# Decode attention over a sliding block of cache: V per group in 64 KB rows, one batch from each of two queues

## The chip, the cores and the metric

One core of a Trainium2 chip. The metric is device time in microseconds of one execution. The kernel before takes 363.2 us (median of 3 runs, 363.07 to 363.21).

## The reference

Two independent problems, A and B, each one decode step of an attention layer, with the results side by side:

```python
B, Sq, D = 2, 1, 576
Hq, Hkv, Sk, Dh = 32, 16, 16384, 128        # W = 4096, rep = Hq // Hkv = 2
q = (x @ wq).reshape(B, Sq, Hq, Dh)          # then heads ahead of Sq
k = repeat(k_cache[:, :, Sk - W:, :], rep)   # the last 4096 positions
v = repeat(v_cache[:, :, Sk - W:, :], rep)
p = softmax(q @ k^T * Dh ** -0.5)
out = (p @ v).reshape(B, Sq, Hq * Dh) @ wo   # 576 columns for each problem
```

All tensors are bf16. K and V of the window are 134 MB in all, wq and wo 9.4 MB each. There is one query row for each head and batch, so every byte of K and V is used for two query heads only.

## The kernel before

**Groups and slabs.** The 16 K/V heads of a problem are taken four at a time: four groups for a problem, eight in all (`NG`), numbered G. A slab is one group, one batch, K or V: 128 partitions of 32 KB, 4,096 KB in all. A partition holds 128 successive positions (`KJ`) of one head, so the 4096 positions of a head lie on 32 partitions. There are 16 K slabs (t = 2G + batch) and 16 V slabs (i likewise).

**Transfers.** `ring` has four slots of one slab. A list `stream` gives the order, K0 K1 K2 K3 V0 K4 V1 and so on, with the output weights (`wo`) as M pieces for groups 0 to 5 and W pieces for the last two. All go from SyncE's queue (L380 for slabs, L364 for wo), each after the last reader of its slot. The last V slab is read in two pieces, the last wo in three.

**Work on a K slab.** `make_X` (L432) turns half a slab in 32 x 32 blocks on DVE into `xt` (two halves, jh = 0 and 1). `make_S` (L442) multiplies it on PE by `zq`, a block layout of the queries that `make_Z` (L414) writes on POOL, into the score tile `st` of the group; a half is 16 matmuls of 512 columns (L462 and, with the weights held, L266). Both batches add into the same tile.

**Softmax of a group.** `make_max` (L468) takes the row maximum on DVE and picks the valid ones on POOL; `make_Tm_pe` (L475) turns it to a row on PE; `make_nM` (L480) reduces it on DVE and scales it on POOL; `make_bias` (L489) turns it back on PE, makes four biases on DVE, and runs four exponentials on ACT (L500), one for each of the four K/V heads, with the sums. `make_pT` (L506) turns the result on DVE into `pT`, which has two buffers. `make_rsum` and `make_sums` (L514, L518) add up the sums and take the reciprocal.

**Work on a V slab.** `make_PV` (L544, matmuls L539) multiplies the V slab by columns of `pT`, as 32 matmuls on tiles of 128 x 32, four of which take the columns of the array side by side. `make_evac` (L553) scales the product out of PSUM and reduces it (L562, L569) on DVE. `make_dg` (L573) on PE and `make_pick` (L582) on DVE bring a group's rows into the layout for the output product, `make_projm` and `make_proj` (L622, L645), whose result `make_E` (L675) writes out.

**Order.** Each engine runs its steps in the order in which the code names them, and waits by semaphores for the others. The loop at L700 goes over K slabs, and what belongs to a group is spread over the slabs that follow, with V three slabs behind K (`LAG`): in the turn of an even t it names X(t,0), the evacuation of V slab t-4, the pick and the maximum of group t/2-1, X(t,1), the row maximum and bias of that group, and the V product of slab t-3; in the turn of the odd t after it X(t,0), an evacuation, pT of that group, X(t,1), its sums, and a V product. So on DVE an X stands between a group's bias and its pT. L741 to L770 write the tail by hand, with `filler` matmuls that compute nothing.

Of the kernel before, what the change touches and what calls it, by code (L numbers as in the profile page):

```python
# [63 lines left out]
def build_kernel(nc, probs, out):  # L64
    NSLOT = 4
    LAG = 3
# [27 lines left out]
    with es:  # L94
# [5 lines left out]
        pR = sb("pR", [128, 2048], BF16)  # L100
        pT = sb("pT", [128, 2, 2048], BF16)
        tmp = sb("tmp", [128, 512], FP32)
        oR = sb("oR", [128, Bb, 128], FP32)
# [4 lines left out]
        ones_f = sb("ones_f", [128, 128], FP32)  # L108
        ones_b = sb("ones_b", [128, 128], BF16)
        sel = sb("sel", [128, 4, 128], BF16)  # L110
        bmask = sb("bmask", [128, 4], FP32)
        vmask = sb("vmask", [128, 4], FP32)
        offm = sb("offm", [128, 4], FP32)
# [4 lines left out]
        m8 = sb("m8", [128, 16, 8], FP32)  # L118
        selx = sb("selx", [128, 8, 16], FP32)
        selm = sb("selm", [128, 16, 8], FP32)  # L120
        bsel = sb("bsel", [128, 2], FP32)
        hmask = sb("hmask", [4, 2], FP32)
        mx = sb("mx", [128, 2], FP32)
        mv = sb("mv", [128, 2], FP32)
        m1 = sb("m1", [128, 1], FP32)
        nM = sb("nM", [1, 16], FP32)
        nMrep = sb("nMrep", [1, 8, 16], FP32)
        bias4 = sb("bias4", [128, 4], FP32)
        rsum4 = sb("rsum4", [128, 4], FP32)
        rsum8 = sb("rsum8", [128, 2, 4], FP32)  # L130
        ssum = sb("ssum", [128, 2], FP32)
        rsb = sb("rsb", [128, 2, 2], FP32)
# [3 lines left out]
        out_w = sb("out_w", [32 + Bb, NH], BF16)  # L136
# [12 lines left out]
        pTf = pT[:].rearrange("p v f -> p (v f)")  # L149
# [3 lines left out]
        assert XW + 512 <= 2 * 2048  # L153
# [5 lines left out]
        ring_sem = [sem("ring%d" % r) for r in range(NSLOT)]  # L159
        v_cuts = [0, 80, KJ]  # L160
        lastv_sem = [sem("lastv")]
# [61 lines left out]
        def turn_x(P):  # L223
# [5 lines left out]
            def f_xT(e, P=P):  # L229
                for k in range(4):  # L230
# [8 lines left out]
        d_dm = mask(dmask[:, 0:4], ident_f[:].rearrange("p (c j q) -> p j c q", j=4, q=8), AX.XY, "dmask")  # L239
# [4 lines left out]
        p_offm = pool(lambda e: e.tensor_scalar(offm[:], vmask[:], -1.0, OFF, ALU.add, ALU.mult), [d_vm], "offm")  # L244
        p_v2 = pool(lambda e: e.tensor_tensor(v2[:], vmask[:, 0:2], vmask[:, 2:4], ALU.add), [d_vm], "v2")
        p_m8 = pool(lambda e: e.tensor_copy(m8[:], jmask_f[:, 0:8].unsqueeze(1).broadcast_to([128, 16, 8])), [d_jf], "m8")
        p_sx = pool(lambda e: e.tensor_copy(selx[:], jmask_f[:, 0:8].unsqueeze(2).broadcast_to([128, 8, 16])), [d_jf], "selx")
        p_sm = pool(lambda e: e.tensor_copy(selm[:].rearrange("p (a h) c -> p a h c", a=2),
                                            jmask_f[:, 0:8].unsqueeze(1).unsqueeze(3).broadcast_to([128, 2, 8, 8])), [d_jf], "selm")
# [72 lines left out]
        stream = []  # L322
        for t in range(NSLAB + LAG):
            if t < NSLAB:
                stream.append(("K", t))
            if t >= LAG:
                i = t - LAG
                if i % 4 == 0 and i > 0:
                    stream.append(("M", i // 4 - 1))
                stream.append(("V", i))  # L330
        stream.append(("W", NG - 2))
        stream.append(("W", NG - 1))
        NM = NG // 2 - 1
        slot_of = {}
        uses = {}
        n_slot = 0
        for key in stream:
            if key[0] in "KV":
                slot_of[key] = (n_slot + 3) % NSLOT
                uses.setdefault(slot_of[key], []).append(key)  # L340
                n_slot += 1
        first_deps = {0: [q_done[0]], 1: [q_done[0], q_done[1]], 2: [q_done[1]], 3: []}
        stream_dma = {}
        last_reader = {}
# [4 lines left out]
        def issue(key):  # L349
# [18 lines left out]
            P, g, b = i // (2 * GP), (i // 2) % GP, i % 2  # L368
            src_t = probs[P][1] if kind == "K" else probs[P][2]
            src = src_t[b, 4 * g:4 * g + 4, Sk - W:Sk, :].rearrange("k (r j) d -> r k j d", j=KJ)  # L370
            r = slot_of[key]
            prior = uses[r][:uses[r].index(key)]
            deps = [last_reader[prior[-1]]] if prior else first_deps[r]
            cuts = [(0, KJ, ring_sem[r])]
            if key == ("V", NSLAB - 1):
                cuts = [(v_cuts[k], v_cuts[k + 1], ([ring_sem[r]] + lastv_sem)[k]) for k in range(2)]
            stream_dma[key] = []
            for c0, c1, sm in cuts:
                def f(e, c0=c0, c1=c1, sm=sm):
                    return e.dma_start(ring[:, r, c0 * 128:c1 * 128],  # L380
                                       src[:, :, c0:c1, :].rearrange("r k j d -> r k (j d)")).then_inc(sm, 16)
                stream_dma[key].append((c0, c1, dma_op("sp", sm, 1, f, deps, "%s%d_%d" % (kind, i, c0))))
# [6 lines left out]
        def filler(n):  # L389
            def f(e):  # L390
                o = STT[(NG - 1) % 2][:, 0:512]
                last = e.matmul(o, ones_b[:, :], xt[:, 0, 0:512], start=True, stop=True, skip_group_check=True)
                for _ in range(n - 1):
                    last = mm_held(e, o, ones_b[:, :], xt[:, 0, 0:512], True)
                return last
            pe(f, [exp_op[NG - 1], Xop[(NSLAB - 1, 1)]], "filler")
# [17 lines left out]
        def make_Z(t):  # L414
            P, g, b = t // (2 * GP), (t // 2) % GP, t % 2
            deps = [qs_ev, p_zq, d_bm]
            if t >= 2:
                deps.append(Sop[(t - 2, 1)])

            def f(e):  # L420
                for kp in range(2):
                    m = 2 * b + kp
                    b0 = zq[:, 0, m, 16 + 4 * m:16 + 4 * m + 1]
                    dst = bass.AP(b0.tensor, b0.offset, [list(b0.ap[0]), [4 * 144, 4], [32, 4], [1, 4]])
                    o = b * Hq + 8 * g + 4 * kp
                    src = qs[:, P, :].rearrange("d (p w) -> d p w", p=4)[:, :, o:o + 4].unsqueeze(2).broadcast_to([128, 4, 4, 4])
                    msk = bmask[:, 0:4].unsqueeze(1).unsqueeze(3).broadcast_to([128, 4, 4, 4])
                    last = e.tensor_tensor(dst, src, msk, ALU.mult)  # L428
                return last
            Zop[t] = pool(f, deps, "Z%d" % t)  # L430

        def make_X(t, jh):  # L432
            ensure(("K", t))
            r = slot_of[("K", t)]
            deps = [stream_dma[("K", t)][0][2], Sop[(t - 1, jh)] if t >= 1 else d_xT[1]]
# [6 lines left out]
        def make_S(t, jh):  # L442
# [3 lines left out]
            if b == 0 and G >= 2:  # L446
                deps.append(exp_op[G - 2])
# [32 lines left out]
        def make_nM(G):  # L480
            n, b = tm_job[G]
            op = ch[(G, "Tm")]
            nm = dve(lambda e: e.tensor_reduce(nM[0:1, 0:16], b[0:1, 0:128].rearrange("o (a w) -> o w a", a=8), AX.X, ALU.max, negate=True),
                     [op] + prev(G, "nMrep"), "nM%d" % G)
            tb_consumer[n] = nm
            ch[(G, "nMrep")] = pool(lambda e: e.tensor_scalar(nMrep[:], nM[0:1, 0:16].unsqueeze(1).broadcast_to([1, 8, 16]), SCALE, None, ALU.mult),
                                    [nm] + prev(G, "bias"), "nMrep%d" % G)

        def make_bias(G):  # L489
            n, bk, op = tb_job(lambda e, bank: e.transpose(bank[:, 0:1], nMrep[0:1].rearrange("o a w -> o (a w)"), ident_f[0:1, 0:1]),  # L490
                               "bias%d" % G, [ch[(G, "nMrep")], p_ident_f])
            ch[(G, "bias")] = op
            b4 = dve(lambda e: e.scalar_tensor_tensor(bias4[:], vmask[:], bk[:, 0:1], offm[:], ALU.mult, ALU.add),  # L493
                     [op, p_offm, d_vm] + ([exp_op[G - 1]] if G >= 1 else []), "bias4_%d" % G)
            tb_consumer[n] = b4
            st = STT[G % 2]

            def f(e):
                for kv in range(4):
                    last = e.activation(pR[:].rearrange("p (x k) -> p k x", k=4)[:, kv, :],  # L500
                                        st[:, :].rearrange("p (x t) -> p t x", t=2)[:, kv % 2, :], ACTF.Exp,
                                        bias=bias4[:, kv:kv + 1], scale=SCALE, accum_out=rsum4[:, kv:kv + 1])
                return last
            exp_op[G] = act(f, [b4] + prev(G, "rsum8") + ([pT_op[G - 1]] if G >= 1 else []), "exp%d" % G)

        def make_pT(G):  # L506
            v = G % 2
            deps = [exp_op[G]] + ([PVop[2 * (G - 2) + 1]] if G >= 2 else [qt_op])
            pT_op[G] = dve(lambda e: e.transpose(  # L509
                pT[:, v, :].rearrange("p (w j q) -> p j w q", w=4, q=8),  # L510
                pR[:].rearrange("p (j w q) -> p j w q", w=4, q=8)), deps, "pT%d" % G)

        def make_rsum(G):
            ch[(G, "rsum8")] = pool(lambda e: e.tensor_tensor(  # L514
# [348 lines left out]
```

## Time and profile before

| | us |
|---|---|
| device time, median of 3 runs | 363.2 |
| device time of the profiled execution | 363.1 |
| span of its instructions | 361.8 |
| PE busy | 229.0 (63%) |
| DVE busy | 218.6 (60%) |
| ACT busy | 45.4 (13%) |
| POOL busy | 24.3 (7%) |
| mean granted TensorE clock | 0.887 |
| moved, mean rate over the span | 153.28 MB, 424 GB/s |

The span runs from the first instruction to the last; the device time has 1.3 us more around it. Busy times are sums over the whole span and don't tell which engine sets the pace of a stretch. A group of instructions is named by line, engine and operation, then what it writes and reads, the shapes and the count; behind it stand the busy time, the mean of one in ns, the idle time before them and who ended it. Matmuls are pipelined and their ends are modelled, so the starts of successive ones tell more than their lengths.

### The profile page before, as it was taken

To read this page: it belongs to the slowest core of one execution; us is meant where nothing else is said; L and a number is where in the kernel's file an instruction comes from. 1 tells how busy PE (TensorE), PEld (TensorE's weight loads), DVE (VectorE), ACT (ScalarE), POOL (GpSimd) and SP (SyncE) were. 2 spreads that over 40 slices of the span, in tenths; PEclk is the share of its full clock that TensorE was granted. 3 is DMA by queue.
4 is the path that set the end of the run, shared out by engine and by line. 5 is a ranking of instruction groups with operands and counts; after the bars stand their busy time and mean duration, and the time that the engine had idled before them with its cause. 6 is when DMAs were issued, how large, how long until landed. Compare 5 with 4: busy or idle time off the path is not lost.

```text
span 361.8 us, 2701 instructions
## 1 busy us (share of the span) xinstructions
PE 229.0 (63%) x1357; PEld 56.1 (16%) x943; DVE 218.6 (60%) x150; ACT 45.4 (13%) x77; POOL 24.3 (7%) x84
## 2 busy tenths in 40 slices
PE   0397687767464866671696656662776675667575
PEld 0010111112110211120121211110112121112222
DVE  0811898495949392924919493952927776675522
ACT  1002100040031002200005000500005000500500
POOL 4200101100010001000010000000010000001000
PEclk9999698969999889888798998899589897869989
DMA  8999999999999999999999999999999999999996
GB/s 327 449 428 420 442 426 424 446 413 446 417 447 420 442 422 422 439 438 420 438 424 434 431 438 412 448 420 442 424 435 429 428 438 420 434 442 420 427 417 258
DMA packets 6088, 153.28 MB, mean 424 GB/s; under 512 B 684, under 2 KB 828, under 8 KB 1084
## 3 DMA queue, kind: packets, MB, share of 16 engines
q1 hardware_dynamic: 6056, 153.10, 98.7%
q8 instruction: 9, 0.15, 0.2%
q14 instruction: 3, 0.02, 0.0%
q10 hardware_dynamic: 20, 0.01, 0.0%
HBM read 153.10 MB, written 0.00 MB: 423 GB/s over the span
## 4 chain that ended last, share of the span: by engine, by line
DMA 49%; DVE 24%; PE 16%; issue 8%; ACT 1%; POOL 1%; SPq 0%
DMA ring<-in_B_k_cache_dram 25%; DVE xt L436 15%; DMA ring<-in_B_v_cache_dram 9%; DMA ring<-in_B_wq_dram 7%; DMA ring<-in_A_k_cache_dram 6%; PE st L266 6%; PE st L462 5%; DMA wob<-in_B_wo_dram 3%; DVE oR L569 2%; DVE mx L470 2%; DVE pT L509 2%; PE pj L266 2%; DVE tmp L562 2%; PE ot L539 1%; ACT pR L500 1%
## 5 line engine op out<-in xcount | busy, mean ns | idle before, releaser
L462 PE MATMUL st<-xt,zq 128*128 128x512 bf16 x256 | 119.3, 466 | 93.6 <-DVE xt L436 93.6
L436 DVE STREAM_TRANSPOSE xt<-ring 128x4096 f32<-128x4096 f32 x32 | 141.6, 4429 | 33.5 <-DMA ring<-in_A_k_cache_dram 18.2
L266 PE MATMUL st<-xt,zq 128*128 128x512 bf16 x256 | 118.0, 461 | 0.0
L500 ACT ACTIVATE pR<-st,bias 128x512 bf16<-128x512 f32 x32 | 40.0, 1419 | 219.0 <-DVE bias L493 219.0
L462 PEld LDWEIGHTS st<-xt,zq 128*128 128x128 bf16 x256 | 28.3, 110 | 211.5 <-DVE xt L436 110.0
L539 PE MATMUL ot<-ring,pT 128*32 128x512 bf16 x512 | 32.0, 393 | 8.3 <-DMA ring<-in_B_v_cache_dram 8.3
L493 DVE SCALAR_TENSOR_TENSOR bias<-vmask,tb,offm 128x4 f32<-128x4 f32 x8 | 1.8, 224 | 37.1 <-PE tb L490 37.1
L523 DVE TENSOR_REDUCE ssum<-tb 128x2 f32<-128x8 f32 x8 | 1.3, 162 | 33.4 <-PE tb L520 33.4
L428 POOL TENSOR_TENSOR zq<-qs,bmask 128x64 bf16<-128x64 bf16 x32 | 8.6, 292 | 161.2 <-PE st L266 140.3
L509 DVE STREAM_TRANSPOSE pT<-pR 128x2048 bf16<-128x2048 bf16 x8 | 18.4, 2303 | 0.7 <-ACT pR L500 0.7
L562 DVE SCALAR_TENSOR_TENSOR tmp<-ot,rsb,dmask 128x512 f32<-128x512 f32 x16 | 11.5, 719 | 9.4 <-PE ot L539 9.4
L281 PE MATMUL ot<-ring,pT 128*32 128x512 bf16 x18 | 7.6, 421 | 15.1 <-DMA ring<-in_A_wq_dram 14.5
L539 PEld LDWEIGHTS ot<-ring,pT 128*32 128x32 bf16 x512 | 12.4, 99 | 23.7 <-DMA ring<-in_B_v_cache_dram 10.5
L569 DVE TENSOR_REDUCE oR<-tmp 128x128 f32<-128x512 f32 x15 | 15.6, 1039 | 0.5
L266 PE MATMUL pj<-ring,pT 128*32 128x512 bf16 x36 | 12.1, 422 | 0.0
L266 PE MATMUL pj<-wob,oM 128*2 128x288 bf16 (+1 forms) x64 | 10.2, 256 | 0.0
L470 DVE TENSOR_REDUCE mx<-st 128x2 f32<-128x1024 f32 x8 | 9.7, 1208 | 0.1
L500 ACT ACTIVATION_READ_ACCUMULATOR pR<-st,bias 128x1 f32 x32 | 9.1, 283 | 0.0
L636 PE MATMUL pj<-wob,oM 128*2 128x288 bf16 x32 | 7.9, 286 | 0.0
L224 DVE TENSOR_TENSOR xt<-xt,hmask 4x1152 bf16<-4x1152 bf16 x2 | 2.8, 1398 | 8.4 <-DMA xt<-in_A_x_dram 8.4
L266 PE MATMUL st<-ring,pT 128*32 128x512 bf16 x18 | 7.4, 414 | 0.0
L472 POOL TENSOR_TENSOR mv<-mx,v 128x2 f32<-128x2 f32 x8 | 1.6, 195 | 80.0 <-DVE mx L470 80.0
(71 smaller groups left out, 79.5 us busy)
## 6 DMA issues: line engine op xcount, KB each, us to landing
ring<-in_A_k_cache_dram SPq DMA_DIRECT2D x8, 4096.0 KB, 24.9
ring<-in_A_v_cache_dram SPq DMA_DIRECT2D x8, 4096.0 KB, 30.0
ring<-in_B_k_cache_dram SPq DMA_DIRECT2D x8, 4096.0 KB, 28.5
ring<-in_B_v_cache_dram SPq DMA_DIRECT2D x7, 4096.0 KB, 31.8
ring<-in_A_wq_dram SPq DMA_DIRECT2D x1, 4608.0 KB, 13.6
ring<-in_B_wq_dram SPq DMA_DIRECT2D x1, 4608.0 KB, 24.1
wob<-in_A_wo_dram SPq DMA_DIRECT2D x2, 2304.0 KB, 29.8
ring<-in_B_v_cache_dram SPq DMA_DIRECT2D x1, 2560.0 KB, 26.9
```

The costliest lines, as they stand in the source:

```text
L266: return e.add_instruction(mybir.InstMatmult(name=nc.get_next_instruction_name(), engine=mybir.EngineType.PE, ins=[e.lower_ap(mv_), e.lowe ...
L281: last = e.matmul(QB[c], wt, mv_, start=first, stop=True, skip_group_check=True)
L428: last = e.tensor_tensor(dst, src, msk, ALU.mult)
L436: Xop[(t, jh)] = dve(lambda e: e.transpose(xt[:, jh, :].bitcast(FP32).rearrange("p (kp x kt) -> p x kp kt", kp=2, kt=2), ring[:, r, jh * H ...
L462: last = e.matmul(ob, wt, mv_, start=first, stop=True, skip_group_check=True)
L470: ch[(G, "max")] = dve(lambda e: e.tensor_reduce(mx[:], st[:, :].rearrange("p (x t) -> p t x", t=2), AX.X, ALU.max), [Sop[(2 * G + 1, 1)]] ...
L500: last = e.activation(pR[:].rearrange("p (x k) -> p k x", k=4)[:, kv, :], st[:, :].rearrange("p (x t) -> p t x", t=2)[:, kv % 2, :], ACTF.Exp,
L509: pT_op[G] = dve(lambda e: e.transpose(pT[:, v, :].rearrange("p (w j q) -> p j w q", w=4, q=8), pR[:].rearrange("p (j w q) -> p j w q", w= ...
L539: last = e.matmul(OTB[32 * c:32 * c + 32, :], pT[:, v, base + 32 * c:base + 32 * c + 32], ring[:, r, jj * 128:(jj + 4) * 128], start=rd == ...
L562: evac_op[i] = dve(lambda e: e.scalar_tensor_tensor(tv, o, rsb[:, v, b:b + 1], dm, ALU.mult, ALU.mult), deps, "ev%d" % i)
L569: ch[(G, "red%d" % b)] = dve(lambda e: e.tensor_reduce(oR[:, b, :], tmp[:].rearrange("p (j d) -> p d j", j=4), AX.X, ALU.add), [evac_op[i] ...
L636: last = e.matmul(PJ[0], oM[:, j, :], mv_, start=start and j == 0, stop=True, skip_group_check=True)
```

## The change

**Layout.** A row is now 256 successive positions, 64 KB, so a head and batch lie on 16 partitions and one group's V of both batches fills the 128 partitions once: batch 0 on partitions 32 to 95, batch 1 on 0 to 31 and 96 to 127. V is read a group at a time (8,192 KB), K as the first or second 128 positions of each row (t = 2G + half), on the same partitions. Batch 0 goes from SyncE's queue, batch 1 from POOL's in two transfers of 32 partitions (`edges`).

**Buffers.** K has two slots (the first slab a place of its own), V one place of two slots; the last V takes the K slots. A V read waits for the V product of the group before, a K read for the X two slabs before. `pT` has one buffer of both batches; the last group's goes to `xt`.

**Work.** The masks become those of the new partitions. Both batches are exponentiated over all partitions, with a bias that leaves out the other batch's, in two steps of four; pT is two transposes. The V product of a group is 64 matmuls on tiles of 128 x 64. There is one evacuation, dg and pick for a group. `rsum8` needs no masking step on POOL any more.

**Order.** The loop goes over groups.

```diff
-    LAG = 3
...
-        pR = sb("pR", [128, 2048], BF16)
-        pT = sb("pT", [128, 2, 2048], BF16)
+        pR = sb("pR", [128, Bb, 2048], BF16)
+        pT = sb("pT", [128, 4096], BF16)
...
+        pT_of = lambda G: pT[:] if G < NG - 1 else xt[:, 0, 0:4096]
+        v_at = lambda G: ringf[:, 2 * SW:4 * SW] if G < NG - 1 else ringf[:, 0:2 * SW]
...
-        v_cuts = [0, 80, KJ]
+        v_cuts = [0, 144, 224, 2 * KJ]
...
+        stream = [("K", 0), ("K", 1), ("M", 0), ("K", 2), ("V", 0)]
+        for G in range(1, NG - 2):
+            stream += [("K", 2 * G + 1), ("K", 2 * G + 2), ("V", G)]
+            if G == 3:
+                stream.append(("M", 1))
+        G = NG - 2
+        stream += [("K", 2 * G + 1), ("K", 2 * G + 2), ("M", 2), ("K", 2 * G + 3), ("V", G), ("V", G + 1)]
+        stream += [("W", NG - 2), ("W", NG - 1)]
+        k_slot = lambda t: 3 if t == 0 else 1 - t % 2
...
+                def f(e, c0=c0, c1=c1, sm=sm):
+                    return e.dma_start(place(key)[32:96, c0 * 128:c1 * 128], piece(key, 0, 0, 16, c0, c1)).then_inc(sm, 16)
+                stream_dma[key].append(dma_op("sp", sm, 1, f, data_deps(key), "%s%d_%d" % (kind, i, c0)))
...
+        def piece(key, b, r0, r1, c0, c1):
+            kind, i = key
+            G = i // 2 if kind == "K" else i
+            o = KJ * (i % 2) if kind == "K" else 0
+            src = probs[G // GP][1 if kind == "K" else 2][b, 4 * (G % GP):4 * (G % GP) + 4, Sk - W:Sk, :].rearrange("k (r j) d -> r k j d", j=2 * KJ)
+            return src[r0:r1, :, o + c0:o + c1, :].rearrange("r k j d -> r k (j d)")
+
+        def data_deps(key):
+            kind, i = key
+            if kind == "K":
+                return ([[], [q_done[0]]][i] if i < 2 else [last_reader[("K", i - 2)]]) + (q_done_all if i == 2 else [])
+            if i == 0:
+                return q_done_all + [last_reader[("K", 0)]]
+            return [last_reader[("K", NSLAB - 2)], last_reader[("K", NSLAB - 1)]] if i == NG - 1 else [last_reader[("V", i - 1)]]
+
+        def edges(key):
...
+                for p0, r0 in ((0, 0), (96, 8)):
+                    def f(e, c0=c0, c1=c1, sm=sm, p0=p0, r0=r0):
+                        return e.dma_start(place(key)[p0:p0 + 32, c0 * 128:c1 * 128], piece(key, 1, r0, r0 + 8, c0, c1)).then_inc(sm, 16)
+                    op = dma_op("pool", sm, 1, f, data_deps(key) if key != ("K", 0) else [wq_dma[1]], "%se%d_%d_%d" % (kind, i, c0, p0))
...
+            for b in range(Bb):
+                def f(e, b=b):
+                    for kv in range(4):
+                        last = e.activation(pR[:, b, :].rearrange("p (x k) -> p k x", k=4)[:, kv, :],
+                                            st[:, :].rearrange("p (x t) -> p t x", t=2)[:, kv % 2, :], ACTF.Exp,
+                                            bias=bias8[:, b, kv:kv + 1], scale=SCALE, accum_out=rsum8[:, b, kv:kv + 1])
+                    return last
+                exp_op[(G, b)] = act(f, [b8] + prev(G, "sums") + ([pT_op[(G - 1, b)]] if G >= 1 else []), "exp%d_%d" % (G, b))
...
+                    for jj in range(c0, c1, 4):
+                        c, h, jh, j = (jj // 4) % 2, jj // KJ, (jj // 64) % 2, jj % 64
+                        base = ((2 * jh + h) * 64 + j) * 16
+                        last = e.matmul(OTB[64 * c:64 * c + 64, :], pT_of(G)[:, base:base + 64], v_at(G)[:, jj * 128:(jj + 4) * 128],
+                                        start=jj < 8, stop=jj >= 2 * KJ - 8, skip_group_check=True)
...
+        def make_K(t, jh):
+            make_X(t, jh)
+            make_S(t, jh)
+
+        edges(("K", 0))
+        edges(("K", 1))
+        make_Z(0)
+        make_Z(1)
+        for jh in range(2):
+            make_K(0, jh)
+        edges(("K", 2))
+        edges(("V", 0))
+        make_Z(2)
+
+        def chain_a(G):
+            make_max(G)
+            make_Tm_pe(G)
+
+        def chain_b(G):
+            make_nM(G)
+            make_bias(G)
+
+        def chain_c(G):
+            make_pT(G, 0)
+            make_pT(G, 1)
+            make_sums(G)
+
+        for k in range(NG - 1):
+            t = 2 * k + 1
+            if k >= 1:
+                make_evac(k - 1)
+            make_K(t, 0)
+            if k >= 1:
+                make_dg(k - 1)
+            make_K(t, 1)
+            edges(("K", t + 2))
+            make_Z(t + 2)
+            if k >= 1:
+                make_pick(k - 1)
+            make_K(t + 1, 0)
+            chain_a(k)
+            make_K(t + 1, 1)
+            chain_b(k)
+            if t + 3 < NSLAB:
+                edges(("K", t + 3))
+                make_Z(t + 3)
...
+            chain_c(k)
+            if k < NG - 2:
+                make_PV(k)
+                edges(("V", k + 1))
         T = NSLAB - 1
...
+        make_K(T, 0)
+        make_K(T, 1)
+        chain_a(NG - 1)
+        chain_b(NG - 1)
+        make_pT(NG - 1, 0)
+        make_pT(NG - 1, 1)
+        make_PV(NG - 2)
+        edges(("V", NG - 1))
+        make_evac(NG - 2)
+        make_dg(NG - 2)
+        make_pick(NG - 2)
+        make_sums(NG - 1)
+        filler(4)
+        make_PV(NG - 1, (0,))
+        filler(4)
+        make_PV(NG - 1, (1,))
+        filler(3)
+        make_PV(NG - 1, (2,))
+        make_evac(NG - 1)
+        make_dg(NG - 1)
+        make_pick(NG - 1)
         make_proj(NG - 2)
         make_proj(NG - 1)
         make_E(NPROB - 1)
```

## The prediction

> **What bounds the kernel now.** I read the page first (span, DMA row, groups), then the busy time by stretch, then the timeline of one group.
>
> ```profile
> span 361.8 us, 2701 instructions
> ...
> DMA  8999999999999999999999999999999999999996
> ...
> q1 hardware_dynamic: 6056, 153.10, 98.7%
> ```
> The transfers are busy from the first slice to the last. By stretch (columns: PE, PEld, DVE, ACT and POOL busy, granted clock, DMA share, GB/s):
> ```profile
> 80.00:120.00 40.00, 24.21 (x146) 5.92 (x106) 28.03 (x15) 5.02 (x8) 2.19 (x8) 0.97 1.01 432
> 200.00:240.00 40.00, 23.89 (x136) 5.99 (x104) 28.04 (x17) 5.00 (x8) 2.19 (x8) 0.91 1.01 432
> ```
> 153.28 MB at 432 GB/s is 354.8 us, so 7.0 of the 361.8 us are start and tail: this kernel is bound by its transfers. A group (four K heads, both batches) takes two K slabs and two V slabs of 4,096 KB, 16.78 MB, or **38.8 us**. No engine needs more than 28 of 40 us, but only because the steps of neighbouring groups overlap:
> ```profile
> 189.20 1.91 PE L539 MATMUL ot<-ring,pT 128*32 128x512 bf16 x32
> ...
> 189.31 0.23 DVE L493 SCALAR_TENSOR_TENSOR bias<-vmask,tb,offm 128x4 f32<-128x4 f32 x1 [8.03 <-PE tb L490]
> 189.45 4.44 DVE L436 STREAM_TRANSPOSE xt<-ring 128x4096 f32<-128x4096 f32 x1
> 189.57 1.45 ACT L500 ACTIVATE pR<-st,bias 128x512 bf16<-128x512 f32 x1 [42.36 <-DVE bias L493]
> ...
> 193.81 0.71 DVE L562 SCALAR_TENSOR_TENSOR tmp<-ot,rsb,dmask 128x512 f32<-128x512 f32 x1
> ...
> 194.27 0.30 ACT L500 ACTIVATION_READ_ACCUMULATOR pR<-st,bias 128x1 f32 x1
> ...
> 195.50 2.30 DVE L509 STREAM_TRANSPOSE pT<-pR 128x2048 bf16<-128x2048 bf16 x1
> ```
> While ACT takes a group's exponentials (189.57 to 194.57, 5.0 us for four), DVE turns the next K half, and PE multiplies an older V slab. The question is what is left of this overlap.
>
> **The change, part by part.**
>
> *Bytes and packets.* The same bytes move. V packets become 64 KB, half the rows now come by POOL's queue. The DMA share already reads 1.01, so I take the rate at 432 and cost this at nothing; the best 9 us slice of the page shows 449, which would save at most 134.2 MB x (1/432 - 1/449 GB/s) = 11.8 us, and only while transfers are the bound.
>
> *Work per group.* The S matmuls are the same 64. Exponentials: each half of the partitions holds one batch, yet both batches are run over all 128, so eight instead of four. pT: two transposes of 2.30 instead of one. V product: the same 64 matmuls of 512 columns, but on tiles 64 wide, so two at a time where four ran. One evacuation instead of two saves 0.72 + 1.04. Counted by engine, DVE gains 2.30 - 1.76 us, ACT 4.7 us: nothing that breaks 38.8 us.
>
> *Order.* The new loop runs, per group k with t = 2k+1: evac(k-1), X(t), pick(k-1), X(t+1,0), max(k), X(t+1,1), chain to the exponentials, pT twice, PV(k). DVE and PE keep their written order. On DVE, pT(k) waits for the exponentials and evac(k) for PV(k), and **X of the next group stands behind both**. On PE, S of the next group stands behind PV(k). Before, a whole X lay under the exponentials; now nothing does but the first pT. So a group becomes one serial loop. Rows used for it:
> ```profile
> L436 DVE STREAM_TRANSPOSE xt<-ring 128x4096 f32<-128x4096 f32 x32 | 141.6, 4429 | 33.5 <-DMA ring<-in_A_k_cache_dram 18.2
> ...
> L562 DVE SCALAR_TENSOR_TENSOR tmp<-ot,rsb,dmask 128x512 f32<-128x512 f32 x16 | 11.5, 719 | 9.4 <-PE ot L539 9.4
> ...
> L569 DVE TENSOR_REDUCE oR<-tmp 128x128 f32<-128x512 f32 x15 | 15.6, 1039 | 0.5
> ...
> L470 DVE TENSOR_REDUCE mx<-st 128x2 f32<-128x1024 f32 x8 | 9.7, 1208 | 0.1
> ```
> ```profile
> 75.94 0.61 PE L462 MATMUL st<-xt,zq 128*128 128x512 bf16 x1 [4.68 <-DVE xt L436]
> ...
> 80.61 0.49 PE L266 MATMUL st<-xt,zq 128*128 128x512 bf16 x1
> 80.94 0.40 PE L462 MATMUL st<-xt,zq 128*128 128x512 bf16 x1
> ...
> 81.65 0.40 PE L266 MATMUL st<-xt,zq 128*128 128x512 bf16 x1
> ```
> After 4.68 us of idle PE, S starts at 0.43 us a matmul and goes to 0.235 after 4.9 us: this half takes 6.1 us, a warm one (181.17 to 185.1) 3.95.
>
> Time from the start of X(t,0), us:
> - X(t,0) 4.43. PE has been idle over 6 us (evacuation and X), so S(t,0) is the cold one: 4.5 to 10.6. dg(k-1), 0.49 in the tail's row: 11.1.
> - pick(k-1) waits for it: product and two reductions, 0.42 + 2 x 0.39 and gaps: 12.4. X(t,1) and S(t,1) (to 15.0) are hidden here.
> - X(t+1,0) 16.8, max 18.0, X(t+1,1) 22.5.
> - S(t+1,1) warm, 26.5; it hides both nM and nMrep steps (0.25 and 0.52 each). From the bias matmul to ACT's start took 189.05 to 189.57: 27.0.
> - Eight exponentials: four start 1.18 apart and end 5.0 after the first, so 9.7: 36.7.
> - pT(k,1) 2.30: 39.1 (the first ran under the second four). Sums matmul 0.3: 39.4.
> - PV(k): 64 matmuls in 32 rounds. A round of four took 1.91/8 = 0.24 us, cold 3.19/8 = 0.40 (the PV at 344.41). PE has idled 12 us, so 3.8 us cold (the rows show 2.6 to 4.9), 9.5 rounds, then 22.5 x 0.236: 9.1, to 48.5.
> - evac and reduction 0.72 + 1.04, 0.2 of handing over: **50.5 us**.
>
> 50.5 against 38.8: the loop, no longer the transfers, sets the pace, and DMA has 11.7 us of slack in each turn. Three checks that nothing else is late. V(k) is issued at the end of PV(k-1), 2 us before this turn, and needs some 20 us; it is wanted at 39.4. The K slab of t+2 goes out at X(t,1)'s end (8.9), t+3 at 22.5; both land behind V by 43 and are wanted at 50.5 and later. POOL's queue: the two issues for t+2 stand ahead of max's follower mult at 18.0 and wait at 8.9; SP shows 0.54 us an issue and no row shows POOL's, so 1.1 us against 9 us of cover (up to 4.5 an issue would hide); those for t+3 follow nMrep, those for V follow PV, where POOL has nothing else due. Without that cover a long issue adds straight to the loop.
>
> *Sum.* Weights land at 25.4 as now. POOL's rows of K0 wait for them and start about 2 us later (27.5; the page's first slice moves 327 of 432 GB/s, which is 2.2 of 9 us); two queues at 216 GB/s each bring K0 at 37.3 and K1 at 47.1. X(1,0) starts there. K2 is issued at X(0)'s end, 46.2, behind the rest of 2.4 MB of wo: 62.5. X(2,0), max, X(2,1), S: 76.5; exponentials to 86.7, pT 89.0, PV and evacuation: turn 1 starts at 100.5. Five turns: 353. Turn 6 to its pT 392.1, sums 0.4, X(15) 401.4, S(15), cold first, 407; max, row maximum and bias 4.5 (330.51 to 334.31 in the tail now, and 1.2 for max): 411.5; exponentials 421.2, pT 423.5, evac(6) with dg and pick 3.8, sums and cold fillers 1.7: 429. V7, issued at 401.4, has landed by 424. PV(7) with seven fillers 10.8: 440. From the last PV's end to the span's end is 6.8 now (355.0 to 361.8): 446.6. The profiled execution took 363.1 for a span of 361.8, so **448 us**, against its own 363.1 and a median of 363.2.
>
> Bounds. PV has no row at this width: four at a time would be 3.8 us (-5.3 a turn, seven turns, -37), one at a time 15 us (+6, +42); two is what 64 of 128 columns leave. Clock: never cold saves 2.2 in S and 1.5 in PV, -26; cold throughout S(t+1,1) and PV adds 2.9 + 3.7, +46. Both ends together are unlikely; the forecast's own range is 410 to 490.
>
> **Rivals.**
> *Half the paths.* POOL moves partitions 0 to 31 and 96 to 127 in two transfers. If each of them, or both, fall on half of the 16 engines or of the ways into the memory while SyncE's rows use all, half of them carry 3/4 of the bytes, and the pair runs at 2/3 of 432, 288 GB/s. A group then takes 58.3 us, more than 50.5. 134.2 MB take 466, after 25.4 of weights, with some 16 for wo and 8 of tail: **515 us**. No row has such a transfer. [...]
>
> *The loop stays hidden* (not slower). If a turn fits in 38.8 us, DMA paces again and the time is 363 less at most 11.8 for longer packets, less than nothing in the tail: **352 to 363**, say 359. For it: all engines have room in sum. Against: PV at four a round and PE never cold give 50.5 - 5.3 - 2.2 = 43.0, still over; only with the exponentials halved too does it decide.
>
> *POOL's issues are dear.* Beyond 4.5 us each they delay mult, and with it the loop; at 8 us each a turn is 7 us longer: 448 + 6 x 7 = 490.
>
> **How the numbers follow.** Forecast 0.72, half the paths 0.12, dear issues 0.06, hidden loop 0.05, a loop between (365 to 405, several bounds low at once) 0.05. Predicted 448. The range 405 to 497 takes the forecast's spread and dear issues. A measurement here can tell 0.2% (0.7 us). Faster 0.05, same 0.01, slower 0.94.
>
> **What would show it.** Right: DMA share near 38.8/50.5 = 0.77 in the middle; exponentials in eights about 50 us apart; DVE's X waiting behind the evacuation, which waits for PE's V product; ACT's eight about 9.7 us, PV about 9 us and starting cold. Half the paths: DMA still full at about 290 GB/s, PV waiting for V. Dear issues: mult waiting behind POOL's queue. Wrong altogether: DMA still at 1.0 and 430 GB/s, groups 39 us apart.

## The result, and the profile after

The changed kernel takes **457.0 us** (median, 456.2 to 457.8) against 363.2 for the kernel before (362.9 to 363.3) on the same chip: **1.258 times as long, 95% interval 1.257 to 1.260**. The forecast was 448 with 405 to 497 as its range. The profiled execution took 457.2 us for a span of 455.6. The times below are medians of all runs of a kernel (four for each variant) and the ratios leave out runs over 1.5% above its fastest, which sets the two apart for the late evacuation alone by more than 0.3%.

The page of the changed kernel, the lines that answer to those of before:

```profile
span 455.6 us, 2879 instructions
...
PE 263.7 (58%) x1359; PEld 77.5 (17%) x945; DVE 225.4 (49%) x156; ACT 82.6 (18%) x141; POOL 58.8 (13%) x171
...
DMA  9999599990899659991999889964999689607960
...
q1 hardware_dynamic: 3384, 85.99, 44.8%
q0 software_dynamic: 4160, 67.12, 34.7%
...
L543 ACT ACTIVATE pR<-st,bias 128x512 bf16<-128x512 f32 x64 | 77.4, 1418 | 314.6 <-DVE bias L536 314.6
...
L415 POOL DMA_DIRECT2D ring<-in_B_v_cache_dram x12 | 6.6, 558 | 64.5 <-PE ot L575 64.3
```

The row of 9s of the DMA engines now has holes from the fifth slice on, and the two queues together hold the engines for 79.5% of the span, not 98.7%. Yet no engine is busy for more than 58% of it. By stretch (columns as before; each is about one turn long):

```profile
100.00:151.00 51.00, 28.03 (x134) 8.70 (x102) 26.78 (x17) 10.70 (x19) 6.09 (x18) 0.77 0.73 312
201.00:252.00 51.00, 27.37 (x134) 8.51 (x102) 27.58 (x18) 10.54 (x18) 6.10 (x18) 0.77 0.78 334
```

The busy sums of PE and DVE are those of before within 4 us per turn; only the stretch they are spread over has grown, and the DMA share reads 0.73 to 0.78. So every engine waits. One turn of the timeline, DVE, ACT and PE, says for whom (start, duration, and in brackets the idle time before and who ended it):

```profile
216.10 8.76 DVE L473 STREAM_TRANSPOSE xt<-ring 128x4096 f32<-128x4096 f32 x2
...
232.65 4.42 DVE L473 STREAM_TRANSPOSE xt<-ring 128x4096 f32<-128x4096 f32 x1
...
241.25 0.23 DVE L536 SCALAR_TENSOR_TENSOR bias<-vm,tb,offm 128x8 f32<-128x8 f32 x1 [3.95 <-PE tb L533]
...
241.51 1.39 ACT L543 ACTIVATE pR<-st,bias 128x512 bf16<-128x512 f32 x1 [39.64 <-DVE bias L536]
...
251.21 2.31 DVE L551 STREAM_TRANSPOSE pT<-pR 128x2048 bf16<-128x2048 bf16 x1 [2.42 <-ACT pR L543]
...
253.58 0.59 PE L557 MATMUL tb<-rsum,m 128*128 128x8 f32 x2 [12.37 <-DVE pT L551]
254.10 8.79 PE L575 MATMUL ot<-ring,pT 128*64 128x512 bf16 x64
...
262.94 0.75 DVE L590 SCALAR_TENSOR_TENSOR tmp<-ot,rsb,dmask 128x512 f32<-128x512 f32 x1 [8.36 <-PE ot L575]
```

Read it as a relay: X to 237.1, the rest of S to the bias at 241.3, ACT alone to 251.2, the second pT, PE alone to 262.9, the evacuation, and only then the next X (264.66, 48.6 us after the first). Turns alternate: those with an output product ahead of the V product are about 2 us longer, and the mean of five is 49.4. While one engine runs, the bracket of the next shows that it stood still: PE 12.4 us for the exponentials, DVE 8.4 us for the V product. The chain of waits of the whole span agrees. Before (first line) the transfers were half of it, now (second line) it goes through all engines and transfers are 14%:

```profile
DMA 49%; DVE 24%; PE 16%; issue 8%; ACT 1%; POOL 1%; SPq 0%
...
PE 38%; DVE 27%; ACT 17%; DMA 14%; issue 2%; POOL 1%; SPq 0%; DVEq 0%; POOLq 0%
```

The start has its own story. DVE's timeline there:

```profile
43.62 8.77 DVE L473 STREAM_TRANSPOSE xt<-ring 128x4096 f32<-128x4096 f32 x2 [23.54 <-DMA ring<-in_A_k_cache_dram]
...
77.24 4.45 DVE L473 STREAM_TRANSPOSE xt<-ring 128x4096 f32<-128x4096 f32 x1 [14.21 <-DMA ring<-in_A_k_cache_dram]
```

K0 and K2 are waited for. Between 30 and 37 us, with both queues full at 435 GB/s together (K rows, and at the end wo's on SyncE's), SyncE's queue (q1) held 61.9% of the engines' time and POOL's 39.3%. Between 60 and 70, when SyncE had gone on to V0 while POOL still read K2, the split was wider (packets, MB, share of the 16 engines):

```profile
q1 hardware_dynamic: 63, 3.34, 77.2%
q0 software_dynamic: 56, 1.05, 24.7%
```

SyncE's half of K2 landed 11.1 us after its issue at 52.4, POOL's two transfers 19.2 us after theirs in the median. So a slab that needs both halves waits for POOL's, while SyncE runs ahead with rows that are not wanted yet.

### The profile page after: what moved, and what is told of

Its sections match the earlier page's. It is cut to its first block, busy times and chain, and to the rows that moved or that the text cites. A ratio compares the mean times of both kernels' runs of the same rounds, so it can differ in the third digit from the quotient of the medians.

```text
span 455.6 us, 2879 instructions
## 1 busy us (share of the span) xinstructions
PE 263.7 (58%) x1359; PEld 77.5 (17%) x945; DVE 225.4 (49%) x156; ACT 82.6 (18%) x141; POOL 58.8 (13%) x171
## 4 chain that ended last, share of the span: by engine, by line
PE 38%; DVE 27%; ACT 17%; DMA 14%; issue 2%; POOL 1%; SPq 0%; DVEq 0%; POOLq 0%
DVE xt L473 18%; ACT pR L543 17%; PE ot L575 14%; PE st L499 11%; PE st L284 10%; DMA ring<-in_A_k_cache_dram 9%; DMA ring<-in_B_wq_dram 5%; DVE pT L551 4%; DVE tmp L590 1%; PE tb L557 1%; DVE mrow L507 1%; DVE oM L631 1%; DVE xt L551 1%; PE tb L605 0%; DVE bias L536 0%
## 5 line engine op out<-in xcount | busy, mean ns | idle before, releaser
L543 ACT ACTIVATE pR<-st,bias 128x512 bf16<-128x512 f32 x64 | 77.4, 1418 | 314.6 <-DVE bias L536 314.6
L575 PE MATMUL ot<-ring,pT 128*64 128x512 bf16 x448 | 64.3, 458 | 0.0
L551 DVE STREAM_TRANSPOSE pT<-pR 128x2048 bf16<-128x2048 bf16 x14 | 32.4, 2312 | 47.7 <-ACT pR L543 47.7
L575 PEld LDWEIGHTS ot<-ring,pT 128*64 128x64 bf16 x448 | 29.0, 131 | 32.0 <-issue 17.2
L465 POOL TENSOR_TENSOR zq<-qs,bmask 128x32 bf16<-128x32 bf16 x64 | 13.2, 233 | 51.0 <-PE st L284 40.7
L543 ACT ACTIVATION_READ_ACCUMULATOR pR<-st,bias 128x1 f32 x64 | 19.0, 297 | 0.0
L299 PE MATMUL ot<-ring,pT 128*32 128x512 bf16 x18 | 7.6, 420 | 15.6 <-DMA ring<-in_A_wq_dram 14.6
L536 DVE SCALAR_TENSOR_TENSOR bias<-vm,tb,offm 128x8 f32<-128x8 f32 x8 | 1.9, 231 | 27.4 <-PE tb L533 27.4
L415 POOL DMA_DIRECT2D ring<-in_A_k_cache_dram x16 | 9.0, 569 | 43.0 <-DVE xt L473 35.6
L415 POOL DMA_DIRECT2D ring<-in_B_k_cache_dram x16 | 8.8, 552 | 38.2 <-DVE xt L473 37.6
L507 DVE TENSOR_REDUCE mrow<-st 128x2 f32<-128x1024 f32 x8 | 9.5, 1189 | 5.0 <-PE st L284 5.0
## 6 DMA issues: line engine op xcount, KB each, us to landing
ring<-in_B_k_cache_dram SPq DMA_DIRECT2D x8, 2048.0 KB, 16.8
```

The lines of the kernel that those rows point to most:

```text
L299: last = e.matmul(QB[c], wt, mv_, start=first, stop=True, skip_group_check=True)
L415: return e.dma_start(place(key)[p0:p0 + 32, c0 * 128:c1 * 128], piece(key, 1, r0, r0 + 8, c0, c1)).then_inc(sm, 16)
L507: ch[(G, "max")] = dve(lambda e: e.tensor_reduce(mx[:], st[:, :].rearrange("p (x t) -> p t x", t=2), AX.X, ALU.max), [Sop[(2 * G + 1, 1)]] ...
L543: last = e.activation(pR[:, b, :].rearrange("p (x k) -> p k x", k=4)[:, kv, :], st[:, :].rearrange("p (x t) -> p t x", t=2)[:, kv % 2, :], ...
L551: pT_op[(G, b)] = dve(lambda e: e.transpose(pT_of(G).rearrange("p (w j b q) -> p b j w q", w=4, b=Bb, q=8)[:, b], pR[:, b, :].rearrange("p ...
L575: last = e.matmul(OTB[64 * c:64 * c + 64, :], pT_of(G)[:, base:base + 64], v_at(G)[:, jj * 128:(jj + 4) * 128], start=jj < 8, stop=jj >= 2 ...
```

## The experiments

The theory: a turn is one chain through DVE, PE and ACT in the written order, about 50 us, and transfers, POOL's issues and packet size have no part in it. The rivals: the transfers (half the paths, or POOL's queue being slow) set the pace, or the turn is sums of busy time. Each edit is made to the changed kernel. Times are medians, each beside the kernel before on the same chip (363.1 to 363.2); the changed kernel's ratio is 1.258. Three dots in a diff stand for lines that aren't shown.

**Less of the transfers: a quarter of V.** From group 1 on only the first quarter of each V row piece is read, 44 MB less.

```diff
+        less = lambda key, c0, c1: c0 + (c1 - c0) // 4 if key[0] == "V" and key[1] >= 1 else c1
...
```

> V of groups 1 to 7 is read to a quarter (44 MB less); the product runs over all columns as before. Theory: the turn isn't set by transfers, 49.4 us stay and the time is 452 to 458 us. Rival (transfers): up to 100 us less, 360 to 420 us.

456.7 us, ratio 1.258 (1.256 to 1.261). A stretch of about one turn, with a piece of wo in it:

```profile
200.00:250.00 50.00, 27.32 (x134) 8.51 (x102) 27.18 (x18) 9.97 (x18) 6.10 (x18) 0.77 0.63 257
```

The DMA share falls from 0.78 to 0.63 here, to 0.52 in the stretch after it, and the time by 0.3 us, which is inside the interval: bytes, their rate and the long packets are worth nothing here. This alone rules out that transfers pace the turns.

**Less of the chain: one batch's exponentials.** Batch 1's four exponentials and its pT are left out.

```diff
-            for b in range(Bb):
+            for b in range(1):
...
```

> Batch 1's exponentials and its pT are left out (constant probabilities and sums in their place); all else stays. Theory: the 4.7 us that ACT needs longer for eight than for four are on the path in each of 8 groups: 457 - 8 x 4.7 = 419 us, 415 to 424. Rival (another step than ACT's is the late one, or transfers): within 1% of 457.

420.4 us, 1.158 (1.156 to 1.160): 36.6 us less, or 4.6 for each of eight groups, where ACT's second four take 4.7. A turn fell from 49.4 to 45.0. ACT is busy for 18% of the span, and yet what it does counts in full, because the steps behind it on the chain wait for it.

**Another order: the evacuation behind the next X.** The evacuation, dg and pick of group k-1 go behind the whole next K slab, so that DVE turns it during the V product.

```diff
-            if k >= 1:
-                make_evac(k - 1)
             make_K(t, 0)
+            make_K(t, 1)
             if k >= 1:
+                make_evac(k - 1)
                 make_dg(k - 1)
-            make_K(t, 1)
             edges(("K", t + 2))
             make_Z(t + 2)
+            make_K(t + 1, 0)
             if k >= 1:
                 make_pick(k - 1)
-            make_K(t + 1, 0)
             chain_a(k)
```

> The order alone: the evacuation of a group stands behind X and S of the next K slab, so X runs under PV. Theory (a turn is one serial loop): X's 8.9 us leave the loop, a turn goes from 49.4 to about 41 us, still over the 38.8 us of its bytes: 457 - 6 x 8.4 = 407 us, 400 to 418. Rival (transfers set the turn, by two queues or by half the paths): the turn stays at 49 us, 450 to 457 us.

429.6 us (423.0 to 430.5), ratio 1.173 (1.164 to 1.183): 27.4 less by the median and about 31 by the ratio, so the order is part of the loss, but the saving falls well short of the 50 that I expected. From bias to bias a turn takes 43 to 45 us most often, once 52. DVE's timeline shows what came in place of the wait that is gone:

```profile
151.63 8.77 DVE L473 STREAM_TRANSPOSE xt<-ring 128x4096 f32<-128x4096 f32 x2 [4.17 <-DMA ring<-in_A_k_cache_dram]
160.33 0.71 DVE L590 SCALAR_TENSOR_TENSOR tmp<-ot,rsb,dmask 128x512 f32<-128x512 f32 x1
162.04 4.43 DVE L473 STREAM_TRANSPOSE xt<-ring 128x4096 f32<-128x4096 f32 x1
```

The evacuation no longer waits for PE, but X waits 4.2 us for its K slab. V has a single place: the next V is read when the V product ends, and the K slab goes out behind it:

```profile
113.55 0.56 SPq L382 DMA_DIRECT2D ring<-in_A_v_cache_dram  x1
114.26 14.94 SPq L382 DMA_DIRECT2D ring<-in_A_k_cache_dram  x2
```

The V product ends at 113.5 us. In the page's slices of 10.7 us the rate is 437 GB/s in the one up to 96 us, 248 and 111 in the next two, up to 118, and 416 to 454 in the three after them, up to 150. With the chain shortened, this buffering is next in line; my 407 had no term for it. No run gave V a second place, so this is read from the timeline and not shown by an edit.

**PE kept busy before the V product.** 44 matmuls that compute nothing stand between S and the V product, in the 12 us (8 where an output product goes ahead) in which PE waits for the exponentials.

```diff
+            if k >= 1:
+                warm(k, 44)
             chain_c(k)
...
```

> 44 matmuls that compute nothing run on PE while ACT takes the exponentials of groups 1 to 6. Theory: PV of groups 1 to 5 then starts at full clock and takes 7.6 instead of about 9.2 us, on the path: 457 - 5 x 1.6 = 449 us, 446 to 452. Rival (the clock costs nothing, PV's 9.2 us are its pace at this width): within 0.5% of 457.

452.2 us, 1.246 (1.243 to 1.249), 4.8 less, just above the expected range. PE's timeline, two turns:

```profile
204.34 7.10 PE L583 MATMUL ot<-ring,pT 128*64 128x512 bf16 x64
...
251.83 8.78 PE L583 MATMUL ot<-ring,pT 128*64 128x512 bf16 x64
```

Where the idle matmuls reach up to the V product, in two of five turns, it takes 7.1 us; the same two took 9.5 without them (204.80 in the changed kernel's timeline, at a granted clock of 0.74). Where 2.8 us of idle time remained ahead of it, it takes 8.8, as without them (254.10 there, at 0.80). Over the profiled span the granted clock is 0.864, against 0.790 without them. Twice 2.4 is about the 4.8 us saved: the cold start of PE is on the path, and 64 matmuls go two at a time (7.1 / 32 = 0.22 us a round), as reckoned.

**The start: SyncE held back.** SyncE's K1 waits for POOL's rows of K0, its V0 for POOL's rows of K2, and the first wo goes behind V0.

```diff
-        stream = [("K", 0), ("K", 1), ("M", 0), ("K", 2), ("V", 0)]
+        stream = [("K", 0), ("K", 1), ("K", 2), ("V", 0), ("M", 0)]
...
+                held = {("K", 1): ("K", 0), ("V", 0): ("K", 2)}.get(key)
...
```

> The start alone: SyncE's K1 waits for POOL's rows of K0, its V0 for POOL's rows of K2, and M0 comes after V0. Theory: K0 is late by 6 us and K2 by 15 because SyncE's queue takes well over half of the engines and runs ahead with what isn't wanted yet; held back, K0 lands at 36 and K2 at 58 to 62, turns stay at 49.4, so 457 - 16 = 441 us, 437 to 446. Rival (POOL's transfers are slow by themselves): K0 still after 41, 452 us or more.

439.7 us, 1.213 (1.208 to 1.219), 17.3 less. The first X and that of the third slab, from DVE's timeline:

```profile
36.00 8.77 DVE L474 STREAM_TRANSPOSE xt<-ring 128x4096 f32<-128x4096 f32 x2 [16.03 <-DMA ring<-in_A_k_cache_dram]
...
58.87 4.45 DVE L474 STREAM_TRANSPOSE xt<-ring 128x4096 f32<-128x4096 f32 x1 [3.18 <-DMA ring<-in_A_k_cache_dram]
```

43.6 became 36.0 and 77.2 became 58.9, and the turns stayed nearly as they were (49.8 in the mean). POOL's first four transfers landed 11.4 us after their issue in the median, not 19.9, so they are not slow by themselves. What was late at the start was POOL's half of a slab, because SyncE's queue took more than half of the engines' time for rows wanted later. What each of the three edits brought was not separated.

**Both orders together.** The late evacuation and the held start.

> The order of e1 and the start of e6 together. Theory: their gains add, 429.6 - 17 = 412 us, 405 to 418, still above the kernel before, since a turn of 41 to 45 us stays (exponentials on the path, and one place for V, whose next read waits for the end of PV).

412.7 us, 1.136 (1.133 to 1.139). The two savings add up, by the medians: 457.0 - 27.4 - 17.3 = 412.3.

**And batch 1's exponentials left out as well.**

> As e9, and batch 1's exponentials and its pT are left out. Theory: a turn then needs about 36 us of steps against 38.8 us of bytes, so transfers bind again: DMA share 0.95 or more in the middle, 372 to 392 us, and the rate of two queues with 64 KB rows shows: 430 GB/s, as before. Rival (rows of 64 KB or two queues cost rate): DMA share near 1 at under 415 GB/s.

401.7 us, 1.103 (1.099 to 1.108), above the 372 to 392 that I expected. Two stretches:

```profile
150.00:200.00 50.00, 35.14 (x186) 10.66 (x128) 31.32 (x22) 4.95 (x8) 7.34 (x24) 0.93 1.00 430
350.00:400.00 50.00, 36.08 (x213) 13.33 (x177) 19.19 (x21) 4.96 (x8) 4.38 (x10) 0.74 0.53 216
```

In the first the transfers are the bound again, at 430 GB/s, the rate of before (432): neither the second queue nor 64 KB rows change it by more than 2 GB/s here. The 4.6 us a turn of the exponentials now bring 11.0 us in all, not 36.6, since X waits for K here (8.9 us at 180.5). The last 50 us run at 53% of the DMA engines: the tail behind the last reads is long in this order.

**All from SyncE's queue.** POOL's two transfers of 32 partitions are issued by SyncE instead, behind its own.

```diff
+            edges_sp(key)
...
-                    op = dma_op("pool", sm, 1, f, data_deps(key) if key != ("K", 0) else [wq_dma[1]], "%se%d_%d_%d" % (kind, i, c0, p0))
+                    op = dma_op("sp", sm, 1, f, data_deps(key), "%se%d_%d_%d" % (kind, i, c0, p0))
...
```

> The queue alone: batch 1's rows go from SyncE's queue behind batch 0's, rows and partitions as changed. Theory: the turn stays at 49.4 us; only the start changes, because K0 and K2 no longer share the engines with what is queued behind them: K0 at 35, K2 at 60 instead of 43.6 and 77.2 us, so 440 to 446 us. Rival (POOL's queue, its issues or its transfers lengthen the turn): turns of 40 us and about 400 us.

603.2 us, 1.660 (1.654 to 1.666): theory and rival both missed, and transfers became part of the path.

```profile
200.00:300.00 100.00, 48.49 (x211) 13.90 (x142) 42.48 (x25) 9.68 (x16) 3.98 (x18) 0.71 0.72 256
```

256 GB/s with the DMA engines at 0.72 is neither full nor free. The rival "half the paths" of the prediction has this shape: were both 8-row transfers on the same half of the engines, that half would carry 3/4 of the bytes, the mean share would be at most 0.67 and the rate 288. That is an estimate on an assumption that no run shows: which engines a transfer took isn't recorded. The measured share lies above that bound and the rate below it, so the account is not complete.

**One transfer of 64 partitions for each batch.** Batch 0 goes to partitions 0 to 63, batch 1 to 64 to 127, in 16 rows each; the masks stay, so the result mixes the batches while the work is the same. First all from SyncE, then from the two queues as in the change.

```diff
-                    return e.dma_start(place(key)[32:96, c0 * 128:c1 * 128], piece(key, 0, 0, 16, c0, c1)).then_inc(sm, 16)
+                    return e.dma_start(place(key)[0:64, c0 * 128:c1 * 128], piece(key, 0, 0, 16, c0, c1)).then_inc(sm, 16)
...
-                for p0, r0 in ((0, 0), (96, 8)):
+                for p0, r0 in ((64, 0),):
...
```

From SyncE alone:

> All from SyncE's queue as in e2, but each batch as one transfer of 16 rows on 64 partitions, 0 to 63 and 64 to 127 (the masks stay, so the result is that of mixed batches; times are of the same work). [...] Rival (transfers to half of the partitions are slow, as for halves of the ways into the memory): about 218 to 290 GB/s and 560 us or more.

From both queues:

> Two queues as changed, but batch 0 on partitions 0 to 63 and batch 1 on 64 to 127, one POOL transfer of 16 rows for two of 8 (masks stay, mixed batches). Theory: turns of 49.4 us hide any rate above 340 GB/s, so 455 to 460 us whatever the partitions do; where the choice of 32 to 95 matters, it shows in the rate of stretches in which both queues work. Rival (partitions 32 to 95 were what kept the rate): under 340 GB/s and over 470 us.

693.4 us, 1.910 (1.903 to 1.916), and 669.3 us, 1.839 (1.829 to 1.849): the rival of each came true, the first at a rate just below the 218 that it gave. A stretch of the first:

```profile
200.00:300.00 100.00, 42.33 (x214) 14.87 (x168) 27.00 (x17) 9.68 (x16) 2.76 (x12) 0.67 1.00 210
```

and of the second:

```profile
200.00:300.00 100.00, 43.19 (x237) 14.71 (x186) 32.57 (x23) 19.34 (x32) 5.32 (x20) 0.73 0.98 219
```

The engines are busy all the time and move half as much. The first K slab isolates the cause: between 25 and 30 us only SyncE's queue moves data, 16 rows of 32 KB for each head in both kernels, to partitions 32 to 95 in the changed kernel (first line) and to 0 to 63 in the one with two queues and halves (second line):

```profile
DMA packets 82, 2.13 MB, mean 426 GB/s; under 512 B 17, under 2 KB 17, under 8 KB 17
...
DMA packets 33, 1.05 MB, mean 210 GB/s; under 512 B 1, under 2 KB 1, under 8 KB 1
```

A packet of 32 KB took 1.21 us there and 2.5 here. So it is the partitions, not the queue and not the row count, that halve the rate here; 32 to 95 for one batch avoids it.

## Why the prediction was right, point by point

**The mechanism.** The forecast said that a group becomes one serial loop longer than its bytes. The turn of 49.4 us, the DMA share, the exponentials in eights and X behind the evacuation show it; the quarter of V and the left-out exponentials show it from both sides.

**The terms of the sum.** Measured against predicted, in us:

| term | predicted | measured | off by |
|---|---|---|---|
| start, to X of turn 1's first slab | 100.5 | 116.65 | +16.15 |
| five turns (116.65 to 363.65) | 252.5 | 247.0 | -5.5 |
| turn 6 and tail, to the span's end | 93.6 | 91.95 | -1.65 |
| span | 446.6 | 455.6 | +9.0 |

That the sum missed by only 9.0 us is in part luck, since 16.15 too little at the start and 7.15 too much in the turns and the tail cancel in part.

**The term mis-sized** is the start: "two queues at 216 GB/s each bring K0 at 37.3 and K1 at 47.1", and K2 after it. Their sum was right (435) and their halves were not: 62 to 39, later 77 to 25. K0 came at 43.6 (+6.3), K2 at 77.2 (+14.7), and the rest of that chain was 1.4 longer. Holding SyncE back brought 36.0 and 58.9, near the 37.3 and 62.5 of the forecast. That the split is so uneven is shown; why POOL's queue gets less is not.

**The turn's steps,** from 216.10, came out 1 to 2 us early all along, mostly from one place: S(t,0), which I took as cold for 6.1 us, was done by about 5.1 us after its X (its matmuls were 0.43 us apart for 2.9 us, where the prediction's row had 4.9), and the early lead is then kept. dg at 9.5 (predicted 11.1), pick done 11.1 (12.4), X(t+1,0) 15.5 (16.8), ACT's start 25.4 (27.0), second pT done 37.4 (39.1), the V product done 46.8 (48.5), end 48.6 (50.5). ACT's eight took 9.7 as reckoned; the V product 8.8 (9.1), or 9.5 behind an output product.

**The rivals.** Half the paths falls for the change as made: 441 GB/s with both queues full at 60 to 70 us, and with SyncE held back POOL's transfers of 8 rows held 97.6% of the engines' time by themselves, at 399 GB/s (30 to 36 us). Rates that pace the turn stood one edit away, though: 256 GB/s with all from SyncE's queue, 210 and 219 with 64 partitions in one transfer. That a transfer falls on half of the engines or of the ways into the memory, which the rival's 288 GB/s and 515 us rest on, no run shows; its chance was the author's estimate. POOL's issues cost 0.56 us each in the page's group above, 1.1 for a pair, and fit the cover of 9 us: POOL stood idle for 2.1 us ahead of the product with the maximum (232.80), waiting for DVE. The hidden loop falls with the DMA share of 0.73 to 0.78.

**The 93.8 us of loss** against the kernel before go back as follows, by the medians and in this order of edits: 27.4 by the order, 16.9 more by the start, 11.0 more by the doubled exponentials, 38.5 left. What is left seems by the traces to lie in V's single place (X waiting for K) and in the long tail; how much in each was not separated. None of these versions reaches the kernel before.

## What to carry to other kernels

Each engine of these kernels took its steps in the written order, so before merging two units of work into one, add up the chain of one turn across engines, not each engine's busy time: here no engine was busy for 60% and the turn still grew from 38.8 to 49.4 us. Splitting a load over two queues gave neither half of the engines here (62 to 39, 77 to 25): hold the one that runs ahead, or the piece that is wanted first comes last. Before moving rows to other partitions, time one transfer on those very partitions, since the same bytes went at 426 or at 210 GB/s here by that alone.

## What the hardware showed that was not expected

- Partitions. Two transfers of 64 partitions, 0 to 63 and 64 to 127, ran at 210 GB/s from SyncE's queue alone and at 219 from two queues in the stretches above, with the DMA engines at 0.98 to 1.0: about half of the 432 GB/s of before. 32 to 95 from SyncE with 0 to 31 and 96 to 127 from POOL ran at 430 (both orders together with half the exponentials, 150 to 200 us), and a first slab to 32 to 95 from SyncE alone at 426. Why the partitions matter, and why two queues for the two halves added only 9 GB/s, no run here shows.
- Eight rows. Two transfers of 8 rows, 32 partitions each, behind one of 16 rows in SyncE's queue, held the engines at 0.72 and gave 256 GB/s. The same shapes from POOL's queue gave 430 to 441 GB/s together with SyncE's 16 rows in the stretches above, and 399 by themselves where SyncE was held back. Why the queue matters, no run here shows.
- Queues. With rows of mostly 32 KB on both, SyncE's queue held 62% of the engines' time and POOL's 39%; with SyncE on rows of 64 KB, 77 and 25%.
